# GpSimd rounds the low words of the first two weight slices, and ScalarE the high half of the first two chunks' activations

## The chip, the cores and the metric

The kernel runs on one core of one Trainium2 chip. The metric is device time in microseconds (us) of one execution; the kernel before takes 623.43 us (median of three runs).

## What is computed

Attention over 4 batches, 8 heads, 768 rows and a head width of 64, with a local window of 96 keys and 8 global keys, and behind it a two-layer block with a GELU between its two products. The weights arrive as 64-bit floats.

```python
def _attn_ref(q, k, v, n_global, n_local) -> np.ndarray:
    ...
    scores = scores + bias[None, :, :, :]
    scores = np.where(keep, scores, -1000000000.0)
    scores = scores - np.max(scores, axis=-1, keepdims=True)
    a = np.exp(scores)
    a = a / (np.sum(a, axis=-1, keepdims=True) + 1e-09)
    return np.matmul(a, v).astype(np.float32)

def _moe_ref(x, w_in, w_out) -> np.ndarray:
    h = x @ w_in
    inv_sqrt2 = np.float32(1.0 / np.sqrt(2.0))
    g = 0.5 * h * (1.0 + erf(h * inv_sqrt2))
    return (g @ w_out).astype(np.float32)
```

`x` is the attention output, 3072 rows of 512; `w_in` is 512 x 2048, `w_out` 2048 x 512.

## The kernel before

**Tiling.** The 3072 rows are 12 chunks of 256 rows (`CT`), three to a batch. The hidden width of 2048 is cut into 8 slices of 256 (`NST`). A step `(c, s)` of `STEPS` multiplies chunk `c` with slice `s` of the first weight (`m1`, tile `h`), applies the GELU (`gelu`, tile `gr`), and adds the product with slice `s` of the second weight to the chunk's sum (`m2`, tile `acc`). Chunks 0 and 1 go through the slices together; from chunk 2 on all slices lie in SBUF. Each fp32 operand is a pair of fp16 tiles, a high half and the rest (`xh`/`xl`, `winh`/`winl`, `wouth`/`woutl`, `gh`/`gl`), and a product is three matmuls: high with high, high with rest, rest with high.

**Weights.** `load_words` brings one of the four pieces of a slice (512 KB, low and high 32-bit words side by side) in tile `w`. `split_weights` makes a float of each double: line 243, on ScalarE, turns the low words into three rounded bits in place; lines 249, 252 and 254, on VectorE, shift the high words (`wb`) and add those bits. `part_weights` one step later writes the high half on ScalarE (line 264) and the rest on VectorE (line 207 in `lo_dve`). A piece's tile is free for the next load once line 254 has read it; SyncE's queue holds those loads.

**Attention of a chunk, by head pair p = 0 to 3.** Score matmuls (`scores_pair`, line 491, tiles `s`); row minimum on VectorE (line 504); exponential with its row sum on ScalarE (line 538, tiles `n` and `su`); sum's reciprocal and scaling (`norm`, lines 547, 550 and 556), for chunks 0 and 1 on VectorE, from chunk 2 on GpSimd; transposes on TensorE (line 578) with a copy on ScalarE (line 583, tile `pt`); the product with v (line 645, tiles `av`), and its two halves `x`, the high one on ScalarE (lines 670, 677), the rest on VectorE (line 206).

**GELU of a step.** Line 835 on ScalarE writes `gr`. For chunks 0 and 1 (`c < CAT`) line 837 on VectorE writes the high half `gh`; for chunks 2 and 3 line 839 on ScalarE does. Line 207 on VectorE writes the rest `gl`.

**What sets the order.** The program is recorded in the order of `run`'s loop over `T`, and a scheduler then places each engine's instructions by its own estimate of their times; `after` adds edges between them without a wait. Line 245 keeps a piece's line 243 behind the piece before the last, line 247 behind the last GELU or exponential (`last_table`). The four pieces of slice 0 are begun at `T` = -5 to -2, those of slice 1 at -1 to 2 (`DECODE`). Up to step (0, 1) TensorE also runs fillers without use (`warm`, `zeros`) that keep it busy.

Of the kernel before, what the change touches and what calls it, by code (L numbers as in the profile page):

```python
# [12 lines left out]
U32 = mybir.dt.uint32  # L13
AF = mybir.ActivationFunctionType
ALU = mybir.AluOpType
# [30 lines left out]
STEPS = [(c, s) for s in range(NST) for c in range(2)]  # L46
# [8 lines left out]
FILL_T = {(1, 6): 6}  # L55
FILL_S = {(1, 1): 0}
LATE = 6
CAT = 2
NEGMASK = -1000000000.0

# [2 lines left out]
GS = 2.0 ** 6  # L63
# [49 lines left out]
class Fast:  # L113
# [115 lines left out]
    def split_weights(self, s, i):  # L229
        nc = self.nc  # L230
        if i == 0:
            if s == LATE:
                self.early.close()
                self.wts = self.ctx.enter_context(self.tc.tile_pool(name="wlate", bufs=1, side="right"))
            if s == NST - 1:
                self.words.close()
                self.wts = self.ctx.enter_context(self.tc.tile_pool(name="wlast", bufs=1))
            for nm, dst, shape in (("win", self.win, [P, 4, 256]), ("wout", self.wout, [P, 2, 512])):
                dst[s] = tuple(self.wts.tile(shape, F16, name=f"{nm}{k}{s}") for k in "hl")
            self.sw[s] = self.wts.tile([P, 2, 4, 256], F16, name=f"sw{s}")  # L240
        w = self.raw.pop((s, i, "w"))
        lw, hw = w[:, :, 0], w[:, :, 1]
        ins = nc.scalar.activation(out=lw, in_=lw.bitcast(U32), func=AF.Copy, scale=2.0 ** -29).ins
        if len(self.his) > 1:
            self.after(ins, self.his[-2], "a piece begins when ScalarE is through with the last but one")
        if self.last_table is not None:
            self.after(ins, self.last_table, "a piece comes behind the exponentials of earlier steps")
        a = self.sm.tile([P, 512], I32, name=f"wb{s}_{i}", tag="o", bufs=3)
        ins = nc.vector.tensor_scalar(out=a, in0=hw, scalar1=0x07FFFFFF, scalar2=3,  # L249
                                      op0=ALU.bitwise_and, op1=ALU.logical_shift_left)  # L250
        self.behind(ins)
        nc.vector.scalar_tensor_tensor(out=a, in0=hw, scalar=-0x40000000, in1=a,  # L252
                                       op0=ALU.bitwise_and, op1=ALU.bitwise_or)
        nc.vector.tensor_tensor(out=a, in0=a, in1=lw, op=ALU.add)  # L254
        self.words_of[s, i] = a
# [365 lines left out]
    def av_pair(self, c, p):  # L621
# [46 lines left out]
        if first:  # L668
            xh, xl = (self.x[c][:, ps.start:ps.stop, e].rearrange("d p (j q) -> d j p q", j=2) for e in range(2))
            nc.scalar.copy(xh, avb)  # L670
            self.lo_dve(xl, avb, xh)
            if p == NP - 1 and c >= CAT:
                self.bounds(self.xtop, self.xlow, self.x[c][:, :, 0, :])
            return
        for j in range(2):
# [3 lines left out]
            if (c, p, j) == (1, NP - 1, 1):  # L679
                self.last_dve = ins  # L680
        if p == NP - 1 and c >= CAT:
            self.bounds(self.xtop, self.xlow, self.x[c][:, :, 0, :])

    def m1(self, t, f):
# [8 lines left out]
        n = 0  # L693
        if s > 1 and c < CAT:
            fs = slice(c * P, (c + 1) * P)
# [131 lines left out]
    def gelu(self, t):  # L827
        nc = self.nc
        if STEPS[t][0] >= SEVEN:
            return self.gelu7(t)  # L830
        hp = self.h.pop(t)
        gh = self.gp.tile([P, 2, CT], F16, name=f"gh{t}", tag="gh")
        gl = self.gp.tile([P, 2, CT], F16, name=f"gl{t}", tag="gl")
        gr = self.gp.tile([P, 2, CT], F32, name=f"gr{t}", tag="gr")
        self.table(nc.scalar.activation(out=gr, in_=hp, func=AF.Gelu, scale=1.0 / (WS * XS)))
        if STEPS[t][0] < CAT:
            nc.vector.tensor_scalar(out=gh, in0=gr, scalar1=GS, scalar2=None, op0=ALU.mult)
        else:
            self.last_table = nc.scalar.activation(out=gh, in_=gr, func=AF.Copy, scale=GS).ins  # L839
        self.last_dve = self.lo_dve(gl, gr, gh, GS).ins  # L840
        self.g[t] = (gh, gl)

    def m2(self, t, k):
# [5 lines left out]
        wh, wl = self.wout[s]  # L849
        if c < CAT and s > 1:  # L850
            for kk in range(2):
# [376 lines left out]
```

## Time and profile before

| what | value |
|---|---|
| runs | 623.43, 624.52, 622.22 us |
| profiled execution | 621.09 us; span of the trace 619.3 us |
| TensorE busy | 599.3 us, 97% of the span |
| VectorE, ScalarE, GpSimd busy | 479.8, 358.6, 81.4 us |
| TensorE's granted clock, mean | 0.99 |
| HBM read, written | 71.83 MB, 6.29 MB |

The span is that of the traced instructions; what lies around it is 1.8 us. PE is TensorE's matmuls, PEld its weight loads, DVE VectorE, ACT ScalarE, POOL GpSimd, SP SyncE; a q behind an engine's name is its queue, where DMAs are issued. An instruction's duration is longer than what it costs its engine in a row of such instructions, since the next begins before the last has ended: where both are at hand, the distance from start to start counts. A granted clock of 1.00 is 2.4 GHz, 0.50 is 1.2 GHz. The page's chain of waits for the whole span begins in the first 120 us with VectorE, ScalarE and DMA, and is TensorE's from there.

### The profile page before, as it was taken

The page shows a single profiled execution, that of the slowest core. Times are in us where ns is not written, and L with a number is a line of the kernel's source. Part 1 is how long each engine was busy: PE and PEld are TensorE (multiplying, and loading weights), DVE is VectorE, ACT ScalarE, POOL GpSimd, SP SyncE. Part 2 cuts the span into 40 slices and gives each one's busy share as a digit, 9 for nine tenths or more (in the row PEclk, how much of TensorE's full clock was granted, in tenths as well). Part 3 has the DMA queues.
Part 4 walks back from the last instruction along what each step waited for, and adds up shares of the span by engine and source line. Part 5 has one row for each costly group of instructions (what it writes and reads, how often), then busy time and mean ns, then how long its engine had stood idle before and what let it go on. Part 6 is the DMA issues. An engine that isn't in the chain of part 4 may idle for free.

```text
span 619.3 us, 19315 instructions
## 1 busy us (share of the span) xinstructions
PE 599.3 (97%) x7896; PEld 457.8 (74%) x7896; DVE 479.8 (77%) x1523; ACT 358.6 (58%) x865; POOL 81.4 (13%) x180
## 2 busy tenths in 40 slices
PE   8987999999999999999999999999999999999995
PEld 5655544455676676788888888888888888889884
DVE  6879999986677785676876876876976876876885
ACT  3777567676547565466466466466466366473331
POOL 1000006211023031022022022022022022020000
PEclk9988999999999999999999999999999999999998
DMA  8958935343261094085185194285285175100001
GB/s 254 249 221 216 293 113 186 109 98 104 71 137 53 37 221 138 37 188 173 36 212 148 36 219 141 71 193 165 73 190 170 70 188 173 62 9 2 36 2 40
DMA packets 111808, 79.46 MB, mean 128 GB/s; under 512 B 54752, under 2 KB 99296, under 8 KB 111712
## 3 DMA queue, kind: packets, MB, share of 16 engines
q1 hardware_dynamic: 109136, 74.47, 43.5%
q10 hardware_dynamic: 2576, 3.67, 1.8%
q8 instruction: 64, 1.05, 0.7%
q14 instruction: 32, 0.26, 0.1%
HBM read 71.83 MB, written 6.29 MB: 126 GB/s over the span
## 4 chain that ended last, share of the span: by engine, by line
PE 77%; DVE 12%; ACT 4%; DMA 2%; issue 2%; SPq 2%; POOL 1%; ACTq 0%; DVEq 0%; POOLq 0%
PE h L704 33%; PE seven L778 23%; PE acc L868 6%; PE av L606 5%; PE s L442 4%; PE h L698 3%; PE acc L853 2%; SPq L318 2%; DVE wb L252 1%; DVE wb L254 1%; DMA kr<-kT 1%; ACT n L538 1%; DVE gl L207 1%; DVE wb L249 1%; POOL n L556 1%
## 5 line engine op out<-in xcount | busy, mean ns | idle before, releaser
L704 PE MATMUL h<-x,winh 128*128 128x256 f16 x1344 | 227.5, 274 | 2.8 <-ACT x L670 1.4
L704 PE MATMUL h<-x,winl 128*128 128x256 f16 x672 | 184.3, 274 | 0.0
L704 PEld LDWEIGHTS <-winh 128*128 128x128 f16 x1344 | 130.4, 98 | 25.3 <-DVE sl L207 3.3
L556 POOL TENSOR_SCALAR n<-n,su 128x160 f32<-128x160 f32 (+1 forms) x160 | 77.9, 509 | 454.4 <-DVE su L550 279.7
L739 ACT ACTIVATE gr<-h 128x512 f32<-128x512 f32 x64 | 38.2, 597 | 94.6 <-PE h L704 92.5
L746 ACT ACTIVATE sh<-ss 128x512 f16<-128x512 f32 x64 | 40.3, 630 | 61.7 <-DVE ss L744 61.7
L744 DVE TENSOR_TENSOR ss<-gr 128x128 f32<-128x128 f32 x128 | 31.3, 285 | 53.9 <-ACT gr L739 53.9
L704 PEld LDWEIGHTS <-winl 128*128 128x128 f16 x672 | 66.1, 98 | 8.8 <-issue 0.8
L207 DVE SCALAR_TENSOR_TENSOR gl<-gr,gh 128x384 f16<-128x384 f32 (+1 forms) x96 | 57.6, 600 | 15.8 <-ACT gh L839 15.4
L778 PE MATMUL seven<-sw,sh 128*128 128x256 f16 x384 | 67.4, 273 | 0.0
L538 ACT ACTIVATE n<-n,mn 128x160 f32<-128x160 f32 x144 | 59.5, 414 | 0.2
L778 PEld LDWEIGHTS <-sh 128*128 128x128 f16 x512 | 48.9, 98 | 6.6 <-issue 0.6
L778 PE MATMUL seven<-sw,sl 128*128 128x256 f16 x192 | 52.3, 273 | 0.5 <-issue 0.4
L207 DVE SCALAR_TENSOR_TENSOR sl<-ss,sh 128x512 f16<-128x512 f32 x64 | 44.2, 691 | 9.4 <-ACT sh L746 9.4
L453 DVE CUSTOM_DVE_ANT_0 n<-s,pens 128x160 f32<-128x160 f32 x144 | 38.0, 320 | 5.2 <-PE s L442 4.0
L778 PEld LDWEIGHTS <-gh 128*128 128x128 f16 x384 | 36.5, 98 | 7.3 <-ACT gr L739 3.3
L538 ACT ACT_TABLE_LOAD x22 | 28.2, 1283 | 13.6 <-DMA qr<-qT 6.9
L778 PE MATMUL seven<-wouth,gh 128*128 128x256 f16 x128 | 35.0, 274 | 0.0
L778 PE MATMUL seven<-wouth,gl 128*128 128x256 f16 x128 | 34.9, 273 | 0.0
L778 PE MATMUL seven<-woutl,gh 128*128 128x256 f16 x128 | 34.9, 273 | 0.0
L606 PEld LDWEIGHTS av<-ptb,vr 32*64 32x64 f32 x2304 | 30.7, 130 | 5.5 <-issue 5.5
L745 ACT ACTIVATE gh<-gr 128x384 f16<-128x384 f32 x64 | 33.5, 523 | 2.1
(161 smaller groups left out, 1134.0 us busy)
## 6 DMA issues: line engine op xcount, KB each, us to landing
w<-w SPq DMA_DIRECT2D x32, 512.0 KB, 6.2
c<-w SPq DMA_DIRECT2D x32, 512.0 KB, 4.0
kr<-kT SPq DMA_DIRECT2D x34, 320.0 KB, 4.7
vr<-v SPq DMA_DIRECT2D x60, 112.0 KB, 2.6
qr<-qT SPq DMA_DIRECT2D x11, 512.0 KB, 4.2
kr<-kT SPq DMA_DIRECT2D x84, 64.0 KB, 4.2
out<-o SPq DMA_DIRECT2D x14, 256.0 KB, 2.3
out<-o ACTq DMA_DIRECT2D x8, 256.0 KB, 2.3
```

The source lines that it names most:

```text
L207: return self.nc.vector.scalar_tensor_tensor(out=out, in0=in_, scalar=scale, in1=hi, op0=ALU.mult, op1=ALU.subtract)
L453: ins = nc.vector.tensor_tensor_reduce(out=nn[:, 2 * hh + u], in0=sp[hh][:, u, :], in1=pens, scale=-0.125, scalar=3e38, op0=ALU.add, op1=A ...
L538: self.table(nc.scalar.activation(out=nn, in_=nn, func=AF.Exp, bias=mn[:, i:i + 1], scale=-1.0, accum_out=su[:, i:i + 1]))
L556: ins = eng.tensor_scalar(out=nn, in0=nn, scalar1=su[:, i:i + 1], scalar2=0.0, op0=ALU.mult, op1=ALU.add)
L606: ins = nc.tensor.matmul(banks[i][hh * D:(hh + 1) * D, u0 * NG:u1 * NG], lhsT=vv[rows, e, b, hh * D:(hh + 1) * D], rhs=g, start=n == 0, st ...
L704: ins = nc.tensor.matmul(hp[:, f, :], lhsT=w[:, d, fs], rhs=x[:, d, e, :], start=n == 0, stop=n == 3 * NP - 1).ins
L739: self.table(nc.scalar.activation(out=gr.rearrange("p i q -> p (i q)"), in_=hp.rearrange("p f q -> p (f q)"), func=AF.Gelu, scale=1.0 / (W ...
L744: self.last_sum = nc.vector.tensor_tensor(out=ss[:, o], in0=x, in1=y, op=op).ins
L745: nc.scalar.activation(out=gh, in_=gr[:, 1:], func=AF.Copy, scale=GS)
L746: self.last_table = nc.scalar.activation(out=sh, in_=ss, func=AF.Copy, scale=GS).ins
L778: ins = nc.tensor.matmul(out, lhsT=g, rhs=w, start=s == 0 and name in ("P1", "P4", "P6", "P3") and i == 0, stop=s >= NST - 4 and i == 2, s ...
L868: ins = nc.tensor.matmul(acc, lhsT=g[:, f, ks], rhs=w[:, f, :], start=s == 0 and n == 0, stop=s == NST - 1 and n == 5).ins
```

## The change

Two things change engines. The low words of slices 0 and 1 (8 pieces of 128 x 512) are scaled on GpSimd and no more on ScalarE, and without the two edges that set their place there; slices 2 to 7 stay as they were. For chunks 0 and 1 (16 steps) `gh` is written by ScalarE and no more by VectorE, so that `last_table` is now that copy.

```diff
+POOLED = 2
...
         lw, hw = w[:, :, 0], w[:, :, 1]
-        ins = nc.scalar.activation(out=lw, in_=lw.bitcast(U32), func=AF.Copy, scale=2.0 ** -29).ins
-        if len(self.his) > 1:
-            self.after(ins, self.his[-2], "a piece begins when ScalarE is through with the last but one")
-        if self.last_table is not None:
-            self.after(ins, self.last_table, "a piece comes behind the exponentials of earlier steps")
+        if s < POOLED:
+            nc.gpsimd.tensor_scalar(out=lw, in0=lw.bitcast(U32), scalar1=2.0 ** -29, scalar2=None, op0=ALU.mult)
+        else:
+            ins = nc.scalar.activation(out=lw, in_=lw.bitcast(U32), func=AF.Copy, scale=2.0 ** -29).ins
+            if len(self.his) > 1:
+                self.after(ins, self.his[-2], "a piece begins when ScalarE is through with the last but one")
+            if self.last_table is not None:
+                self.after(ins, self.last_table, "a piece comes behind the exponentials of earlier steps")
...
         self.table(nc.scalar.activation(out=gr, in_=hp, func=AF.Gelu, scale=1.0 / (WS * XS)))
-        if STEPS[t][0] < CAT:
-            nc.vector.tensor_scalar(out=gh, in0=gr, scalar1=GS, scalar2=None, op0=ALU.mult)
-        else:
-            self.last_table = nc.scalar.activation(out=gh, in_=gr, func=AF.Copy, scale=GS).ins
+        self.last_table = nc.scalar.activation(out=gh, in_=gr, func=AF.Copy, scale=GS).ins
         self.last_dve = self.lo_dve(gl, gr, gh, GS).ins
```

The scheduler then orders the first 150 us anew. Three places follow; the numbers behind a tile's name only tell tiles of one name apart, and lines above 241 are some lines further down in the changed file.

ScalarE, from chunk 0's last products with v (`x<-av_3`) to chunk 1's third exponentials (`n_2`). Before:

```order
L264 ACTIVATE wouth_327<-wb_2_446 128x512
L538 ACTIVATE n_1_542,su_1_531<-n_1_542,nmax 128x192 x4
L243 ACTIVATE w_0_206<-w_0_206 128x512
L264 ACTIVATE wouth_327<-wb_3_505 128x512
L670 CAST x<-av_3_520 128x256
L583 COPY pt_0_586<-t_0_582 128x384
L583 COPY pt_0_586<-t_1_606 128x384
L583 COPY pt_2_648<-t_2_644 128x384
L583 COPY pt_2_648<-t_3_650 128x384
L835 ACT_TABLE_LOAD
L835 ACTIVATE gr_602<-h_569 128x512
L538 ACT_TABLE_LOAD
```

Now:

```order
L268 ACTIVATE wouth_327<-wb_2_446 128x512
L674 CAST x<-av_3_520 128x256
L542 ACTIVATE n_1_542,su_1_531<-n_1_542,nmax 128x192 x2
L587 COPY pt_0_586<-t_0_582 128x384
L542 ACTIVATE n_1_542,su_1_531<-n_1_542,nmax 128x192
L587 COPY pt_0_586<-t_1_606 128x384
L542 ACTIVATE n_1_542,su_1_531<-n_1_542,nmax 128x192
L268 ACTIVATE wouth_327<-wb_3_505 128x512
L839 ACT_TABLE_LOAD
L839 ACTIVATE gr_602<-h_569 128x512
L840 ACTIVATE gh_600<-gr_602 128x512
L542 ACT_TABLE_LOAD
```

The cast of `x<-av_3` has moved ahead of the four exponentials, line 243's piece is gone, the two copies of `pt_2` come behind `n_2`, and `gh` stands between the GELU and the next table load.

VectorE, at the same place, from slice 0's fourth piece (`wb_3`) on. Before:

```order
L249 TENSOR_SCALAR wb_3_505<-w_3_186 128x512
L207 SCALAR_TENSOR_TENSOR woutl_328<-wb_2_446,wouth_327 128x512
L252 SCALAR_TENSOR_TENSOR wb_3_505<-w_3_186,wb_3_505 128x512
L504 ISA n_1_542,nmax<-s_2_532,pens 128x192
...
L254 ISA wb_3_505<-w_3_186,wb_3_505 128x1024
L547 TENSOR_SCALAR su_1_531<-su_1_531 128x4
L550 RECIPROCAL su_1_531<-su_1_531 128x4
L556 TENSOR_SCALAR n_1_542<-n_1_542,su_1_531 128x192 x4
L249 TENSOR_SCALAR wb_0_565<-w_0_206 128x512
L207 SCALAR_TENSOR_TENSOR woutl_328<-wb_3_505,wouth_327 128x512
L206 TENSOR_TENSOR x<-av_3_520,x 128x256
```

Now:

```order
L253 TENSOR_SCALAR wb_3_505<-w_3_186 128x512
L508 ISA n_1_542,nmax<-s_2_532,pens 128x192
...
L208 SCALAR_TENSOR_TENSOR woutl_328<-wb_2_446,wouth_327 128x512
L256 SCALAR_TENSOR_TENSOR wb_3_505<-w_3_186,wb_3_505 128x512
L207 TENSOR_TENSOR x<-av_3_520,x 128x256
L258 ISA wb_3_505<-w_3_186,wb_3_505 128x1024
L508 ISA n_2_622,nmax<-s_4_612,pens 128x192
...
L551 TENSOR_SCALAR su_1_531<-su_1_531 128x4
L554 RECIPROCAL su_1_531<-su_1_531 128x4
L560 TENSOR_SCALAR n_1_542<-n_1_542,su_1_531 128x192 x4
```

The four reductions of `n_1` (one row shown) come before the two weight instructions, `x<-av_3` before the scaling of `n_1` and no more behind it, and the reductions of `n_2` as well.

GpSimd, its first instructions behind the constants. Now (before, the last row shown came right behind the first):

```order
masks.py:199 AFFINE_SELECT ident<-ident 128x128
L245 TENSOR_SCALAR w_0_180<-w_0_180 128x512
L245 TENSOR_SCALAR w_1_182<-w_1_182 128x512
L245 TENSOR_SCALAR w_2_184<-w_2_184 128x512
L245 TENSOR_SCALAR w_3_186<-w_3_186 128x512
L245 TENSOR_SCALAR w_0_206<-w_0_206 128x512
L245 TENSOR_SCALAR w_1_208<-w_1_208 128x512
L245 TENSOR_SCALAR w_2_210<-w_2_210 128x512
L245 TENSOR_SCALAR w_3_212<-w_3_212 128x512
L560 TENSOR_SCALAR n_0_1136<-n_0_1136,su_0_1125 128x192 x4
```

The eight pieces stand in the order of their loads, and behind them the first scaling of chunk 2.

## Rows read from the trace of the kernel before

**Rows 1.** The page, part 1: busy time, share and count by engine.

```profile
PE 599.3 (97%) x7896; PEld 457.8 (74%) x7896; DVE 479.8 (77%) x1523; ACT 358.6 (58%) x865; POOL 81.4 (13%) x180
```

**Rows 2.** Windows: length; PE, PEld, DVE, ACT, POOL busy; granted clock, DMA share, GB/s.

```profile
38.00:39.00 1.00, 1.00 (x6) 0.73 (x5) 1.00 (x7) 0.84 (x1) 0.00 (x0) 0.50 0.24 94
...
45.00:60.00 15.00, 12.68 (x119) 9.43 (x118) 13.79 (x39) 11.92 (x29) 0.00 (x0) 0.89 0.72 170
...
75.00:90.00 15.00, 15.00 (x95) 6.81 (x93) 15.00 (x36) 8.30 (x14) 0.00 (x0) 1.00 0.53 169
```

**Rows 3.** Chain of waits, 20 to 45 us: start, length, work.

```profile
21.20 2.22 DMA kr<-kT
...
37.07 2.83 PE h L704 x14
...
41.83 1.87 ACT n L538 x8
```

**Rows 4.** Timeline of ScalarE, 34 to 36 us: start, length, instruction.

```profile
34.20 0.64 ACT L243 ACTIVATE w<-w 128x512 int32<-128x512 uint32 x1
...
35.26 0.35 ACT L670 CAST x<-av 128x256 f16<-128x256 f32 x1
```

**Rows 5.** Timeline of VectorE, 30 to 62 us.

```profile
30.50 0.42 DVE L249 TENSOR_SCALAR wb<-w 128x512 int32<-128x512 int32 x1
...
32.03 0.35 DVE L504 CUSTOM_DVE_ANT_0 n<-s,pens 128x192 f32<-128x192 f32 x1
...
36.60 0.42 DVE L206 TENSOR_TENSOR x<-av,x 128x256 f16<-128x256 f32 x1
...
44.15 1.01 DVE L556 TENSOR_SCALAR n<-n,su 128x192 f32<-128x192 f32 x4
...
49.52 1.01 DVE L556 TENSOR_SCALAR n<-n,su 128x192 f32<-128x192 f32 x4
...
60.93 0.69 DVE L207 SCALAR_TENSOR_TENSOR gl<-gr,gh 128x512 f16<-128x512 f32 x1
```

**Rows 6.** Groups by line and form: busy us, mean ns; idle before, releaser.

```profile
L556 POOL TENSOR_SCALAR n<-n,su 128x160 f32<-128x160 f32 x144 | 63.1, 461 | 355.8 <-DVE su L550 274.5 <-ACT n L538 81.2
...
L252 DVE SCALAR_TENSOR_TENSOR wb<-w,wb 128x512 int32<-128x512 int32 x32 | 22.0, 692 | 0.0
...
L243 ACT ACTIVATE w<-w 128x512 int32<-128x512 uint32 x32 | 20.3, 673 | 3.2 <-DMA w<-w 3.2
L556 POOL TENSOR_SCALAR n<-n,su 128x192 f32<-128x192 f32 x16 | 14.8, 941 | 98.6 <-ACT n L538 93.4 <-DVE su L550 5.3
...
L839 ACT ACTIVATE gh<-gr 128x512 f16<-128x512 f32 x16 | 10.1, 630 | 0.5
...
L837 DVE TENSOR_SCALAR gh<-gr 128x512 f16<-128x512 f32 x16 | 7.1, 445 | 5.3 <-ACT gr L835 5.3
```

**Rows 7.** Timeline of GpSimd in chunk 2's first scaling: its first instruction, all eight.

```profile
95.81 2.60 POOL L556 TENSOR_SCALAR n<-n,su 128x192 f32<-128x192 f32 x1 [93.36 <-ACT n L538]
...
95.81 9.77 POOL L556 TENSOR_SCALAR n<-n,su 128x192 f32<-128x192 f32 x8 [93.36 <-ACT n L538]
```

**Rows 8.** Timeline of VectorE, with GpSimd idle (first) and at work.

```profile
67.35 0.69 DVE L207 SCALAR_TENSOR_TENSOR woutl<-wb,wouth 128x512 f16<-128x512 f32 x1
...
100.69 0.82 DVE L207 SCALAR_TENSOR_TENSOR gl<-gr,gh 128x512 f16<-128x512 f32 x1
101.44 0.68 DVE L252 SCALAR_TENSOR_TENSOR wb<-w,wb 128x512 int32<-128x512 int32 x1
```

**Rows 9.** Timeline of TensorE: matmuls that waited, in brackets how long.

```profile
61.68 0.39 PE L868 MATMUL acc<-wouth,gl 128*128 128x512 f16 x1 [0.97 <-DVE gl L207]
...
101.03 0.44 PE L578 MATMUL t<-ident,n 128*128 128x128 f32 x2 [0.76 <-POOL n L556]
```

**Rows 10.** Tile w on SyncE's queue, 25.5 to 26 us: slice 1's first load.

```profile
L217 SPq DMA_DIRECT2D w<-w x1: 593/593/593, 25.6 to 25.6; - x1
...
DMA to landing us min/median/max: 6.0/6.0/6.0
```

## The prediction

> **What bounds the kernel now.** The page's first part comes first: TensorE is busy 97% of the span [rows 1], so a gain can only come from a stretch in which it waits or idles on fillers. The windows show which. From 75 to 90 us TensorE and VectorE are both busy for all 15.00 us; from 45 to 60 TensorE has 12.68, VectorE 13.79 and ScalarE 11.92, and the granted clock's mean is 0.89, because it stands at 0.50 (1.2 GHz) in two short stretches, one of them around 38 us [rows 2]. So the stage to look at ends at some 62 us; behind it TensorE has its matmuls one upon the other. In that stage the chain of waits runs from a DMA (chunk 1's keys, landed at 23.42) through VectorE and ScalarE, with 14 products of `h` on TensorE between them [rows 3]. It ends at 61.68, where TensorE waits 0.97 us for `gl` of step (0, 1) [rows 9].
>
> **What is removed and added.** ScalarE loses 8 pieces of 0.67 us and gains 16 copies `gh` of 0.63, VectorE loses 16 of 0.45 [rows 6]: ScalarE's sum grows by 16 x 0.63 - 8 x 0.67 = 4.7 us, VectorE's shrinks by 7.1. Neither sum is a time. All eight pieces and three of the copies lie in the stage before 62 us; the other copies lie beside a full TensorE, where a VectorE that is relieved by 0.45 us a step shortens nothing. GpSimd gains 8 pieces. No DMA is added or moved past another.
>
> **Up to 23.4 us: nothing.** Chunk 0's chain can be up to 1 us shorter without two pieces on ScalarE, but chunk 1's scores start when its keys land [rows 3], and no part of the change touches SyncE's queue ahead of them. I take 0.
>
> **From 23.4 to 62 us: 4.0 us gained.** The new order on VectorE starts from line 249 at 30.50 [rows 5]. The four reductions of `n_1` follow at once, then lines 207 and 252, then `x<-av_3`: 0.4 + 4 x 0.35 + 2 x 0.69 by the durations puts it at 33.7, some 33.2 from start to start, instead of 36.60 [rows 5, 6, 8]. Its high half on ScalarE no longer stands behind four exponentials (1.87 us [rows 3]) and the pieces of lines 243 and 264 (1.06, from 34.20 to 35.26 [rows 4]), so it is there at about 32.3. The last 14 products of `h` then begin at 33.3 to 33.8 instead of 37.07. They took 2.83 us at the low clock [rows 3], half of that at the high one: they end between 35.0 and 36.6 instead of 39.90, and the GELU, behind the last piece of slice 0 and a table load, comes at 36.0 to 36.6, 3.3 to 3.9 us earlier. Now `gh` stands behind it on ScalarE, 0.63 us at most. So the exponentials of `n_2` start at 38.4 to 39.0 instead of 41.83. VectorE in the new order does the reductions of `n_3` and a weight instruction before it scales `n_2` (42.2 to 42.8 instead of 44.15), but that work stood behind the scaling before. With one 249, one 207, one 252 and one 254 (2.2 us) and the scaling of `n_2` (1.01) after it, `n_3` is scaled at 45.5 to 46.1 instead of 49.52. From there to `gl` at 60.93 VectorE has the same instructions but for line 837 [rows 5]. I take 4.0 us, where the steps give 3.4 to 4.3.
>
> **GpSimd's pieces: 1.0 us given back.** No row shows a piece of 512 columns on GpSimd. By columns, the 144 scalings of 160 columns (461 ns) give 1.5 us, the sixteen of 192 (941 ns) 2.5 us, and the slowest of them, 2.60 us, 6.9 us [rows 6, 7]. I take 2.5, since VectorE is as busy here as beside those sixteen. Slice 1's first piece lands at 31.6 [rows 10]; four pieces end at some 42, before VectorE wants the second one's bits. Behind the pieces on GpSimd's queue stand only chunk 2's scalings, 50 us later [rows 7]. So the pieces block nobody by their length, but they slow VectorE: beside GpSimd line 207 took 0.82 instead of 0.69, while line 252 stayed at 0.68 against a mean of 0.692 [rows 6, 8]. From 31.6 to 42 the new order has three of line 207, one 249 and four scalings of `n_1`: 8 x 0.13 = 1.0 us. If VectorE is waiting for ScalarE anyway, it is 0. The Trainium skill (SBUF — State Buffer, section "Who interferes with whom") has a harder rule: VectorE and GpSimd lock a shared port pair for a whole instruction, and an instruction with two SBUF inputs waits for it. By it the pieces would cost more than 1.0; the rows show VectorE lose 0.13 and GpSimd wait up to 2.60, so here it is mostly GpSimd that pays.
>
> **From 62 us on: nothing, between 1 lost and 1 gained.** Two table changes, before chunk 2's exponentials, get a `gh` in front, 0.5 us each, on the way to the scalings for which TensorE waited 0.76 at 101.03 [rows 9]. Against that, a VectorE with less to do gives GpSimd its turn sooner. From chunk 4 on nothing is changed.
>
> **The sum.** 0 - 4.0 + 1.0 + 0 = -3.0 us against the profiled execution's 621.09: 618.1. That execution lies 2.3 us below the median of the three runs, 623.43, so in medians 620.4. With the bounds (gain 3.4 to 4.9, the larger if the clock stays high; 0 to 1.5 given back; 1 either way behind 62 us), not all at their ends at once, the forecast reaches from 618.0 to 621.9. A half per cent of 623.43, about what a measurement tells from no change, is 3.1 us: the border of faster is at 620.3, in the middle of the forecast.
>
> **Rivals.**
> *The gain is spent again.* VectorE is full from 75 us on [rows 2]; if TensorE, started 3 us earlier, then waits for weights that VectorE or the loads cannot bring earlier, the time is 622 to 624. For it: with VectorE at 15.00 there is no slack in sight. Against it: VectorE itself runs ahead by the same 3 us and loses 0.45 us of work a step, and its tiles, and with them the loads, come free earlier.
> *The lock.* If each of slice 1's four pieces stops VectorE for its length (1.5 us, the 461 ns of 160 columns scaled to 512), that is 6.0 us instead of 1.0: +2.0 in place of -3.0, so 625.4. This is what the lock of the skill's SBUF page would do. Against it: line 252 was not slowed at all.
> *The pieces are slow.* If a piece takes 6.9 us as the slowest row gives, slice 0's four, begun at some 13 us (an estimate: their loads are ahead of chunk 1's keys on SyncE's queue), end at 41, slice 1's at 68. The last of these goes into `wouth` for TensorE's `acc` of step (0, 1), forecast for 58.5; with 254, 264 and 207 behind it, that comes some 9 us late, against a forecast that was 3.0 early: +6, so 629.4. It decides from about 5.5 us a piece on, where slice 1 ends at 57. For it: 32-bit integers in and out, which no GpSimd row shows. Against it: the slowest of the rows is one that waited, not one that worked.
> *More than forecast.* If both stretches of low clock go and the waits of 0.97 and 0.76 with them [rows 9], 1.4 + 0.97 + 0.76 = 3.1 more: 617.3.
>
> **Chances.** Forecast 0.60, half of it on either side of 620.3; gain spent again 0.14; lock 0.06; slow pieces 0.07; more than forecast 0.13. Faster by over 0.5%: 0.30 + 0.13 = 0.43. Within: 0.30 + 0.14 + 0.06 = 0.50. Slower: 0.07. The range from 617.2 to 624.5 holds the forecast, the spent gain and the larger gain, and leaves out lock and slow pieces, 0.13.
>
> **What would show it.** GpSimd rows of line 245, 128x512, near 2.5 us each, the last of slice 1 ended before 45 us; the cast of `x<-av_3` near 32 and the GELU of step (0, 0) near 36.5; the scaling of `n_3` near 46; TensorE's first `acc` with `gl` of step (0, 1) near 58.5 instead of 61.68; and then no wait of more than 1 us on TensorE up to 150. It is wrong if line 245 takes over 4 us, if VectorE's idle time ends on GpSimd, if line 207 takes over 0.9 us between 32 and 42, or if TensorE, early at 62, is no longer early at 130.

## The result and the profile after

The changed kernel takes 627.2 us (median of 8 runs, 624.57 to 633.55) where the kernel before takes 621.25 in the runs beside them: a ratio of 1.0098, 95% interval 1.0071 to 1.0125. It is slower by 6 us; the forecast was 620.4, within 617.2 and 624.5. The profiled execution took 628.27 us with a span of 626.4, 7.1 more than before.

Line numbers are up to 4 higher in the changed kernel (207 is 208, 243 is 247, 252 is 256, 254 is 258, 419 is 423, 425 is 429, 504 is 508, 556 is 560, 835 is 839), and in the kernels of the experiments they can be a few higher still (835 is 840 in e1 and 842 in e5). The page's busy times say little, as [rows 1] did before: ScalarE has 5 us more, VectorE 4 less, GpSimd 8 more, TensorE 2 more.

```profile
PE 601.4 (96%) x7896; PEld 457.3 (73%) x7896; DVE 475.6 (76%) x1507; ACT 363.9 (58%) x873; POOL 89.4 (14%) x188
```

The windows find the place. The first fence is the kernel before, the second the changed one; columns as in [rows 2].

```profile
105.00:120.00 15.00, 15.00 (x134) 7.42 (x133) 15.00 (x36) 10.30 (x22) 2.04 (x8) 1.00 0.36 132
120.00:135.00 15.00, 14.51 (x73) 7.17 (x72) 14.37 (x56) 9.58 (x22) 5.43 (x11) 1.00 0.73 166
135.00:150.00 15.00, 15.00 (x171) 8.23 (x170) 8.55 (x33) 11.83 (x32) 3.04 (x8) 1.00 0.11 34
```

```profile
45.00:60.00 15.00, 12.74 (x155) 9.56 (x155) 14.95 (x42) 12.46 (x30) 0.00 (x0) 1.00 0.83 196
75.00:90.00 15.00, 15.00 (x92) 6.73 (x91) 15.00 (x35) 9.09 (x16) 0.00 (x0) 1.00 0.48 159
...
105.00:120.00 15.00, 14.42 (x132) 7.15 (x130) 15.00 (x37) 12.23 (x27) 2.10 (x9) 1.00 0.17 49
120.00:135.00 15.00, 9.26 (x44) 4.40 (x43) 8.15 (x44) 10.91 (x27) 4.14 (x8) 0.84 0.71 146
135.00:150.00 15.00, 15.00 (x126) 6.67 (x124) 6.14 (x27) 8.88 (x24) 2.23 (x6) 0.93 0.01 2
```

Between 120 and 135 us TensorE falls from 14.51 us to 9.26, and the granted clock is below 1 there and in the next window. What it waits for stands in its timeline of the changed kernel, with the row that answers to the first of [rows 9]:

```profile
61.49 0.39 PE L869 MATMUL acc<-wouth,gl 128*128 128x512 f16 x1 [0.90 <-DVE gl L208]
...
133.58 1.01 PE L702 MATMUL h<-x,winh 128*128 128x512 f16 x2 [5.74 <-ACT gr L839]
134.39 0.63 PE L702 MATMUL h<-x,winl 128*128 128x512 f16 x1
...
137.18 0.59 PE L702 MATMUL h<-x,winh 128*128 128x512 f16 x2
137.61 0.38 PE L702 MATMUL h<-x,winl 128*128 128x512 f16 x1
```

TensorE stands still for 5.74 us until a GELU frees a bank. Behind that the same products last 1.01 and 0.63 us where a little later they last 0.59 and 0.38: windows of half a microsecond show the clock at 0.50 (1.2 GHz) for 6.8 us between 130 and 137, so for the 3.4 us of them in which TensorE works again, half speed costs some 1.7 us more. The GELU is late because of what ScalarE does ahead of it. Its timeline, before and then changed:

```profile
125.12 1.20 ACT L264 ACTIVATE wouth<-wb 128x512 f16<-128x512 f32 x2
126.34 1.28 ACT L835 ACT_TABLE_LOAD   x1
127.63 0.60 ACT L835 ACTIVATE gr<-h 128x512 f32<-128x512 f32 x1
...
128.49 0.61 ACT L835 ACTIVATE gr<-h 128x512 f32<-128x512 f32 x1
...
132.77 4.05 ACT L425 ACTIVATE pens<-rb 128x640 bf16<-128x640 f32 x8 [3.30 <-DVE rb L419]
136.73 0.58 ACT L835 ACTIVATE gr<-h 128x512 f32<-128x512 f32 x1
```

```profile
124.94 1.13 ACT L268 ACTIVATE wouth<-wb 128x512 f16<-128x512 f32 x2
127.57 4.05 ACT L429 ACTIVATE pens<-rb 128x640 bf16<-128x640 f32 x8 [1.49 <-DVE rb L423]
131.64 1.28 ACT L839 ACT_TABLE_LOAD   x1
132.93 0.60 ACT L839 ACTIVATE gr<-h 128x512 f32<-128x512 f32 x1
```

The eight scalings of `scale_pens` (`pens`, the penalties that chunks 3 to 11 use) stood behind two GELUs, the 13th and 14th of the program, those of steps (0, 6) and (1, 6). The scheduler now puts them ahead of both, and they first wait 1.49 us for VectorE's `rb`: 1.49 + 4.05 = 5.54 us, nearly all of TensorE's 5.74. Neither `scale_pens` nor `more_pens`, which makes `rb`, is in the diff. The expectations below call these two the GELUs of chunk 2; what runs beside them is chunk 2's attention, while chunk 2's own first GELU comes at 153.67 before. The two belong to the 16 steps whose `gh` the change moves.

And the 3 us that the start was to bring? In this execution TensorE reaches the product on `gl` of step (0, 1) at 61.49 instead of 61.68. It is not clear from one profile whether GpSimd's pieces took the gain or something else did.

### The profile page after: what moved, and what is told of

The parts are those of the page before. It is cut to its first block, busy times and chain, and to the rows that moved or that the text cites. A ratio compares the mean times of both kernels' runs of the same rounds, so it can differ in the third digit from the quotient of the medians.

```text
span 626.4 us, 19308 instructions
## 1 busy us (share of the span) xinstructions
PE 601.4 (96%) x7896; PEld 457.3 (73%) x7896; DVE 475.6 (76%) x1507; ACT 363.9 (58%) x873; POOL 89.4 (14%) x188
## 4 chain that ended last, share of the span: by engine, by line
PE 72%; DVE 15%; ACT 8%; issue 3%; DMA 1%; SPq 0%; ACTq 0%; DVEq 0%
PE h L708 32%; PE seven L782 23%; PE acc L869 5%; PE av L610 5%; PE s L446 4%; ACT n L542 3%; DVE wb L256 2%; DVE wb L258 2%; DVE gl L208 1%; DVE n L508 1%; DMA kr<-kT 1%; ACT L839 1%; DVE wb L253 1%; DVE n L560 1%; DVE winl L208 1%
## 5 line engine op out<-in xcount | busy, mean ns | idle before, releaser
L560 POOL TENSOR_SCALAR n<-n,su 128x160 f32<-128x160 f32 (+1 forms) x160 | 72.3, 476 | 431.0 <-DVE su L554 344.1
L702 PE MATMUL h<-x,winh 128*128 128x512 f16 x96 | 30.4, 394 | 5.9 <-ACT gr L839 5.9
```

The costliest lines, as they stand in the source:

```text
L560: ins = eng.tensor_scalar(out=nn, in0=nn, scalar1=su[:, i:i + 1], scalar2=0.0, op0=ALU.mult, op1=ALU.add)
L702: nc.tensor.matmul(hp, lhsT=w[:, d, fs], rhs=self.xs[:, 0:2, d, e, :], start=d == 0 and i == 0, stop=d == NP - 1 and i == 2)
```

## The experiments

Three theories: the order of the penalties on ScalarE is the loss; the pieces on GpSimd slow VectorE at the start; ScalarE is overloaded by the high parts wherever the penalties stand. The first four runs set them apart.

**e1.** The penalties are recorded at `T` = 16, not 14 and 15, and held behind the GELU and its copy before them:

```diff
-            if PENS < T < PENS + 3:
-                self.scale_pens(T - PENS - 1)
+            if T == PENS + 3:
+                for k in range(2):
+                    self.scale_pens(k)
...
+            self.after(ins, self.last_table, "behind the activations of earlier steps")
```

> The changed kernel with one edit: the eight scalings that make the second set of penalties are held behind the second GELU pair of chunk 2, where they stood before. Theory (the order on ScalarE at 127 us): the idle of 5.7 us and the some 1.7 us that the products lose at the low clock right behind it go, so 627.2 - 7.4 = 619.8 us, and TensorE shows no wait over 1 us between 125 and 145. Rival (the new load on ScalarE, 14 of 15 us busy there, is the cause, and 4 us of scalings hurt wherever they stand): 624 to 626 us, with a wait on a GELU some steps later. Rival (the pieces on GpSimd cost the time at the start): 626 to 627 us.

620.18 us (618.35 to 622.15, 10 runs), ratio to before 0.9979 (0.9962 to 0.9996): 7.0 us come back. TensorE's longest waits between 62 and 160 us are now 1.03 and 0.57. ScalarE's timeline in its trace, and then TensorE's:

```profile
36.64 0.60 ACT L840 ACTIVATE gr<-h 128x512 f32<-128x512 f32 x1
...
122.85 1.28 ACT L840 ACT_TABLE_LOAD   x1
124.15 0.60 ACT L840 ACTIVATE gr<-h 128x512 f32<-128x512 f32 x1
...
127.05 3.34 ACT L429 ACTIVATE pens<-rb 128x640 bf16<-128x640 f32 x6
```

```profile
19.47 0.43 PE L650 MATMUL av<-pt,vr 128*64 128x128 f32 x2 [0.82 <-DVE su L555]
...
58.21 0.39 PE L870 MATMUL acc<-wouth,gl 128*128 128x512 f16 x1 [0.90 <-DVE gl L208]
```

The last of these rows is a finding of its own: 58.21, 3.5 us ahead of before [rows 9]. Up to the penalties, all engines of this kernel have the changed kernel's order, instruction for instruction, pieces included.

**e2.** The kernel before, with both `scale_pens` recorded at `T` = 14 and the GELU held behind them:

```diff
+            self.last_table = ins
...
-            if PENS < T < PENS + 3:
+            if T == PENS + 1:
```

> The kernel before with one edit: the eight scalings are put ahead of the first GELU of chunk 2. Theory (the order alone costs it): TensorE waits 5 to 6 us for that GELU near 128 us, and the time is 621.2 + 7.4 = 628.6 us. Rival (the order costs only where ScalarE also makes the high parts): 621 to 623 us.

630.47 us (4 runs), ratio 1.0139 (1.0105 to 1.0173). The order alone makes the kernel before slower, without any piece on GpSimd. The price is higher than expected, 9.1 us: the wait is 6.46 us, and the clock stays at 0.50 for 10.2 us instead of 6.8, of which TensorE works for 6.3, so half speed costs some 3.1 us.

```profile
136.72 0.87 PE L579 MATMUL t<-ident,n 128*128 128x128 f32 x3 [6.46 <-ACT gr L836]
```

**e3, e4.** Each half of the change alone (`POOLED = 0`; line 837 back on VectorE).

> The changed kernel with the low words on ScalarE again: only the move of the high parts is left, and the scheduler puts the penalties behind the first GELU pair. Theory: at the start no gain and none of the slower VectorE, so the first product on gl of step (0,1) between 61 and 63 us; the second GELU of chunk 2 comes up to 4 us late, of which TensorE covers some 3: 622 to 624 us. Rival (contention of GpSimd is the cause of the loss): 620 us or less.

> The changed kernel with the high parts on VectorE again: only the pieces on GpSimd are left, and the penalties stand behind the second GELU as before. Theory: VectorE loses some 3 to 4 us beside the pieces and ScalarE's 5 us are gained, so at 62 us within 1 us of before, and 620 to 622 us in all. Rival (contention of GpSimd is the cause of the loss): 624 us or more.

e3: 624.24 us, ratio 1.0041 (1.0019 to 1.0063). No gain at the start (first GELU at 40.14, before 39.92), and the penalties stand between the 13th and the 14th GELU, which comes at 135.56 instead of 128.49. TensorE's 49th product of `wouth` with `gl` starts when it did before (132.75, before 132.71), the 57th 2.2 us later (141.53, before 139.34). e4: 619.87 us, ratio 0.9977 (0.9953 to 1.0001), penalties where they were, first GELU at 36.75, product on `gl` at 58.58. So GpSimd's part is the one that brings the start forward, and it does not need the high parts, though e4's interval just reaches no change; the high parts alone, with the order that they bring, cost 2.8 us in medians. Only together do they bring the penalties ahead of both GELUs.

**e5.** e1 with every piece followed by a twin on GpSimd:

```diff
+            twice = self.sm.tile([P, 512], F32, name=f"tw{s}_{i}", tag="tw", bufs=1)
+            nc.gpsimd.tensor_scalar(out=twice, in0=lw, scalar1=1.0, scalar2=None, op0=ALU.mult)
```

> The kernel of e1 with a second GpSimd instruction of the same shape behind each of the eight pieces, into a scratch tile that nothing reads; the other engines keep their order. Theory (GpSimd's pieces slow VectorE beside them): VectorE's instructions between 12 and 40 us lose some 2 to 3 us more, the first GELU comes 1 to 2 us later than the 36.6 us of e1, and the time is 621 to 622.5 us. Rival (the pieces are free to VectorE): 620.2 us and the GELU at 36.6.

620.03 us (12 runs), ratio 0.9977 (0.9962 to 0.9993): no different from e1. GpSimd does slow VectorE, but the median does not show it. In the profiled execution (621.35, the second slowest of the twelve) the first GELU comes at 37.15, 0.5 later than in e1, and the product on `gl` at 59.77, 1.6 later, with the clock at 0.50 for 3.4 us from 39.7 on, which e1 does not have. VectorE by groups from 11 to 45 us, before, e1 and e5:

```profile
L504 DVE CUSTOM_DVE_ANT_0 n<-s,pens 128x192 f32<-128x192 f32 x18 | 5.7, 354 | 0.4 <-PE s L491 0.4
L556 DVE TENSOR_SCALAR n<-n,su 128x192 f32<-128x192 f32 x20 | 5.5, 315 | 0.1
...
L252 DVE SCALAR_TENSOR_TENSOR wb<-w,wb 128x512 int32<-128x512 int32 x5 | 3.4, 686 | 0.0
L556 DVE TENSOR_SCALAR n<-n,su 128x128 f32<-128x128 f32 x8 | 2.3, 284 | 0.1
...
L207 DVE SCALAR_TENSOR_TENSOR winl<-wb,winh 128x512 f16<-128x512 f32 x2 | 1.4, 687 | 0.0
```

```profile
L561 DVE TENSOR_SCALAR n<-n,su 128x192 f32<-128x192 f32 x20 | 7.2, 397 | 0.0
L509 DVE CUSTOM_DVE_ANT_0 n<-s,pens 128x192 f32<-128x192 f32 x22 | 6.9, 347 | 0.6 <-PE s L496 0.6
L256 DVE SCALAR_TENSOR_TENSOR wb<-w,wb 128x512 int32<-128x512 int32 x6 | 4.4, 732 | 0.0
...
L561 DVE TENSOR_SCALAR n<-n,su 128x128 f32<-128x128 f32 x8 | 2.5, 310 | 0.1
...
L208 DVE SCALAR_TENSOR_TENSOR winl<-wb,winh 128x512 f16<-128x512 f32 x3 | 2.0, 682 | 0.0
```

```profile
L563 DVE TENSOR_SCALAR n<-n,su 128x192 f32<-128x192 f32 x18 | 7.2, 431 | 0.0
L511 DVE CUSTOM_DVE_ANT_0 n<-s,pens 128x192 f32<-128x192 f32 x22 | 6.9, 348 | 0.0
L258 DVE SCALAR_TENSOR_TENSOR wb<-w,wb 128x512 int32<-128x512 int32 x5 | 4.2, 843 | 0.0
...
L208 DVE SCALAR_TENSOR_TENSOR winl<-wb,winh 128x512 f16<-128x512 f32 x2 | 1.8, 906 | 0.0
```

The scalings of `n` go from 315 ns to 397 and 431, line 252 from 686 to 732 and 843, line 207 from 687 to 682 and 906; reductions that read scores from PSUM stay at 350.

**e6, e7.** e1 with only one slice's pieces on GpSimd (`POOLED = 1`; `if s == 1`).

> The kernel of e1 with only slice 0's pieces on GpSimd, slice 1's on ScalarE. Theory (ScalarE is what the start waits for): the first GELU stays at 36.6 us, the four pieces of 0.67 us between 31 and 50 us put off the exponentials and the casts there, and the first product on gl of step (0,1) comes 1 to 2.5 us later than the 58.2 us of e1: 621 to 622.5 us. Rival (slice 1's pieces slow VectorE as much as they help ScalarE): 620 us.

> The kernel of e1 with only slice 1's pieces on GpSimd, slice 0's on ScalarE. Theory: slice 0's pieces on ScalarE put off the copies and casts from 17 to 33 us by up to 2.7 us, less what VectorE gets back: first GELU near 38.5 us, 621 to 622 us. Rival (GpSimd beside VectorE is what costs in slice 0, and TensorE's wait at 19.5 us brings the low clock): the GELU at 36 us and 618.5 to 619.5 us.

e6: 618.83 us (12 runs), ratio 0.9964 (0.9947 to 0.9981), the best of all and below both kernels; its interval overlaps those of e1 and e4. The product on `gl` comes at 58.78, 0.6 later than in e1 and not 1 to 2.5. The rival held: no gain of slice 1's pieces on GpSimd shows, and VectorE has e1's order to the end of the program. e7: 625.09 us (6 runs), ratio 1.0068 (1.0045 to 1.0091), outside both expectations. In its profiled execution (622.18, the fastest of the six) TensorE waits 2.39 us at 50.29 for a scaled `n`, and the GELU of step (0, 1) comes at 59.84, 6.0 later than in e1. The scheduler reordered VectorE and ScalarE from the start in this one, so it prices an order and not the pieces of slice 0 alone.

**e8.** e1 with `(0, 2, 1): 8` in `FILL` instead of 4.

> The kernel of e1 with four more products on zeros ahead of the wait for su at 19.5 us (0.82 us there, 1.24 in the changed kernel's profile, where a low clock of 3.4 us began 0.7 us behind it). Theory (that wait lets the clock fall in some of the runs): the wait is below 0.3 us, the granted clock of the runs lies at 0.995 or above, and the median falls to 618.6 to 619.6 us. Rival (the filler delays the products behind it, or the clock falls elsewhere): 620 to 621.5 us.

620.24 us (12 runs), ratio 0.9992 (0.9978 to 1.0006): the rival. The clock did rise (0.994 to 0.998 over the runs, e1 0.990 to 0.997), but VectorE's order changed too: TensorE now waits 0.93 us for that at 20.77, and the first GELU comes at 38.95, though the clock never falls between 5 and 170 us.

**e9, e10.** What makes up the 7 us? e9 is the changed kernel with the line `self.after(...)` of e1 only, which takes the four narrow scalings behind the GELU. e10 is the changed kernel with `(2, 5): 24` in `FILL_T`, 24 products on stale `x` in the wait.

> The changed kernel with the four narrow scalings (0.45 us each) held behind the GELU, the four wide ones (0.72 us each) still ahead of it. Theory (each us of scalings ahead of the GELU is a us of TensorE): the wait of 5.74 us becomes 4.2 to 4.4 us, the low clock behind it still comes, and the time is 627.2 - 1.5 = 625.7 us. Rival (the wait is for VectorE's base of the penalties, whatever stands behind it): 627 us.

> The changed kernel with 24 idle products (128x384, written to a bank that the transposes then overwrite) on TensorE in the stretch in which it waits for the GELU. Theory (5.7 us of the loss are idle and 1.7 us are the low clock that the idle brings): no low clock between 130 and 140 us, the products on h behind the wait at full speed, and 627.2 - 1.7 = 625.5 us. Rival (the clock falls whatever TensorE does there, or the filler is in the way): 627 to 628 us.

e9: 626.23 us (4 runs, 625.14 to 628.55), ratio 1.0095 (1.0065 to 1.0125); the wait is 4.47 us, 1.27 less for 1.5 us less of scalings, as expected; the time lies between the two expectations. e10: 624.94 us (5 runs, 624.03 to 627.87), ratio 1.0072 (1.0042 to 1.0101), near the 625.5 expected, but not as cleanly as thought: the filler lasts 4.06 us, waits of 1.86 and 0.53 remain, and a stretch of 3.4 us at 0.50 still follows.

```profile
124.72 4.06 PE L520 MATMUL t<-x 128*128 128x384 f16 x24
...
130.97 0.38 PE L703 MATMUL h<-x,winh 128*128 128x512 f16 x1 [1.86 <-ACT gr L840]
```

**e11.** e6 with the high parts back on VectorE and no edit to the penalties.

> The kernel of e6 without the high parts on ScalarE: only slice 0's low words are on GpSimd, and the penalties stand behind the second GELU by the scheduler's own order. Theory (the gain at the start comes from slice 0's low words off ScalarE alone): 618.5 to 619.9 us, first GELU between 36.6 and 37.5 us. Rival (the high parts give VectorE room that the gain needs): 621 us.

619.53 us (12 runs), ratio 0.9973 (0.9959 to 0.9987), first GELU at 37.55: four pieces of slice 0 off ScalarE, with the order that the scheduler makes of that, are enough for the gain. It is the kernel before with the new branch in `split_weights` and `POOLED = 1`, and nothing else.

## Why the prediction was wrong

**The step that failed** is "From 62 us on: nothing, between 1 lost and 1 gained", with, in the part on what is added, "a VectorE that is relieved by 0.45 us a step shortens nothing". I looked at what the edited instructions do there, and not at what the scheduler does with their neighbours. In place of nothing the runs show a wait of 5.74 us and some 1.7 us at half speed near 130 us, of which e1 takes back 7.0. VectorE in the changed order has `rb` done earlier, ahead of `gh` and `gl` of the 13th GELU and no more behind them. VectorE before, and then changed:

```profile
130.04 0.41 DVE L837 TENSOR_SCALAR gh<-gr 128x512 f16<-128x512 f32 x1
...
131.35 0.69 DVE L207 SCALAR_TENSOR_TENSOR gl<-gr,gh 128x512 f16<-128x512 f32 x1
132.08 0.66 DVE L419 TENSOR_SCALAR rb<-rb 64x960 f32<-64x960 f32 x1
```

```profile
126.88 0.66 DVE L423 TENSOR_SCALAR rb<-rb 64x960 f32<-64x960 f32 x1
```

The eight scalings, which need `rb`, now stand earlier on ScalarE, ahead of a GELU that TensorE needs. As recorded, the first four (`T` = 14) stand ahead of that GELU in both kernels; before, it was the scheduler that put them behind it. That the scheduler did this because it reckoned with a relieved VectorE is argued and not shown: no run records its estimates. What shows is that the scalings move with the high parts on ScalarE (the changed kernel and e3) and stay without them (e4 and e11). ScalarE's order in that stretch, written out, would have told it in advance: 4.05 us of scalings ahead of a GELU, where TensorE is busy for 14.5 of 15 us, were there to be priced. e1 and e2 show both directions: taking the order back gains 7.0 us, bringing it into the kernel before loses 9.1.

**From 23.4 to 62 us, right in e1's profiled execution.** In e1, the changed kernel's own order at the start, every landmark lies within 0.4 us of its forecast range: the rest of `x<-av_3` at 33.53 (forecast 33.2), the GELU at 36.64 (36.0 to 36.6), the exponentials of `n_2` from 39.22 (38.4 to 39.0), its scaling at 42.97 (42.2 to 42.8), that of `n_3` at 46.33 (45.5 to 46.1), the product on `gl` at 58.21 (58.5). Of the lead, 3.1 us are there at the rest of `x<-av_3`, before the clock of the kernel before first falls, so the order makes it and not the clock. It lasts: the GELUs between 195 and 480 us come 3.7 earlier than before.

**GpSimd's pieces, a term with a wrong shape.** They take 1.66 us, not 2.5:

```profile
L245 POOL TENSOR_SCALAR w<-w 128x512 int32<-128x512 uint32 x8 | 13.3, 1664 | 22.6 <-DMA w<-w 22.2
...
L560 POOL TENSOR_SCALAR n<-n,su 128x192 f32<-128x192 f32 x16 | 9.0, 582 | 67.2 <-DVE su L554 63.2 <-PE t L582 4.0
```

VectorE pays not 0.13 on each of eight instructions but most on the scalings of `n`: 20 x 0.082 + 8 x 0.026 = 1.9 us from 11 to 45 us, and nothing on line 207 (0.69 in e1 at 32.33). Line 252, for which I read no loss, pays 6 x 0.046 = 0.3: one of the six takes 1.00 us. Slice 0's stretch, for which I took 0, is among it. Since e5 doubles the load and the median stays, the price on the path is below the 1 us or so that the intervals leave open; 1.0 is neither shown nor refuted.

**The size of the start's gain in medians.** Profiled, e1 is 2.7 us shorter in span than before; in medians 1.2 (620.18 against 621.4), where 3.0 was forecast. Two things lie between. e1's profiled execution, 618.35, is the fastest of its ten, and of the 25 runs of the kernel before beside it two took 618.18 and 618.50, so one profiled pair does not give the medians. And its lead is 3.8 us up to the issue of the last output (609.84 against 613.65); only the time from there to the end of the span is longer, 6.7 us against 5.7. Five profiled executions have this start (e5 with its twins). In two of them, the changed kernel and e9, the clock stands at 0.50 for 3.4 us between 20.5 and 25, and the first GELU comes at 39.93 and 38.93; in e1, e10 and e5 it does not fall there, and the GELU comes at 36.64, 37.26 and 37.15. TensorE of the changed kernel, and of e1:

```profile
20.24 0.43 PE L649 MATMUL av<-pt,vr 128*64 128x128 f32 x2 [1.24 <-DVE su L554]
20.60 1.39 PE L495 MATMUL s<-kr,qr 64*128 64x128 f32 x12
21.92 2.07 PE L526 MATMUL warm_ps<-wz 128*128 128x512 f32 x4
```

```profile
19.84 0.98 PE L496 MATMUL s<-kr,qr 64*128 64x128 f32 x12
20.74 1.19 PE L527 MATMUL warm_ps<-wz 128*128 128x512 f32 x4
```

With a low stretch at this place the first GELU comes 1.7 to 3.3 us later; up to 0.8 of that is there before the clock falls (the first row above starts at 20.24, in e1 at 19.47). That is where the profiled run of the changed kernel lost its start. I allowed for a clock that stays high, not for one that falls earlier. That this explains the other medians is argued from the five profiles; the remaining runs give only a mean clock, and e8, whose clock rose while its time did not fall, does not support it. How much of the forecast 3.0 us the start is worth in a usual run stays open.

**The base.** The forecast in medians stood on 623.43, the median of three runs; the eight beside the changed kernel give 621.25. Three us below that is 618.3.

**The rivals.** The spent gain did not come: TensorE was not short of weights. Of the larger gain, e1 has the high clock from 5 to 170 us and no wait near 101, but the wait for `gl` stays, 0.90 at 58.21; its profiled 618.35 is not 617.3. Slow pieces (1.66 us against the 5.5 from which that rival decides) and the lock fell too. By the lock VectorE would be shut out for whole instructions of GpSimd; the largest loss of one instruction here is 0.48 us (line 252 takes 1.164 at 33.08 in e5, beside a piece, where its mean before is 0.686), so an instruction of GpSimd does not hold VectorE for its 1.66 us. The chance of 0.07 on slower was put on the wrong mechanism. Of the signs named in advance, "no wait of more than 1 us on TensorE up to 150" was the one that counted. The last one came with it: 0.2 us early at 62, the changed kernel's TensorE gets its 13th GELU 5.3 us late (132.93 against 127.63).

## What to carry to other kernels

Where a scheduler orders the engines, an edit's price includes every instruction it moves: compare the orders to the program's end, and price each one that now stands ahead of something the bounding engine waits for. A free slot that a relieved engine gets can be filled with work that hurts another engine. Pinning such work behind its critical neighbour (the few lines of e1) was worth more than the change itself.

## What the runs showed of the hardware

- A standstill of TensorE of 5.7 to 6.5 us brought 6.8 to 10.2 us at 0.50 of the clock; standing 4.47 us (e9) brought 3.4. Waits of 1.24 and 1.29 us at 20 us were followed by 3.4 us at 0.50, while e6 and e11 waited 1.30 there and kept 1.00. Before the change, 3.4 us at 0.50 followed waits of 1.41 (35.66) and 1.99 (49.89); e11 waited 1.52 at 42.28 and kept 1.00. What decides is open.
- GpSimd's speed goes with VectorE's load. Chunk 2's first eight scalings took 9.77 us before [rows 7] and 4.88 in the changed kernel, where VectorE has 1.8 us less to do between 90 and 105; in e4, with the high parts back on VectorE, GpSimd's mean for this form (128x192) is 896 ns again, against 582. Whether the amount of VectorE's work or its kind decides is not separated.
- Beside GpSimd, VectorE's scalings from SBUF to SBUF get longer, by 26% on the mean in e1 and 37% in e5. Lines 252 and 207, with two SBUF inputs, get longer by 7% and not at all in e1, by 23 and 32% in e5; the reductions that read PSUM do not (354, 347, 348 ns). The Trainium skill (SBUF — State Buffer, section "Who interferes with whom") names the same kinds, VectorE's `tensor_scalar` and its instructions with two SBUF inputs; the trace agrees on which contend, and differs on how hard: none of them lost more than 0.48 us beside a GpSimd instruction of 1.6 us.
